# Attention products of two heads in the two halves of the TensorE array, with a transposed output that is turned back

## Chip, cores, metric

One core of one Trainium2 chip. The metric is the device time of one execution in microseconds, the median of several; every run named below was fast, and each kernel was compared with runs of the kernel before on the same chip.

## The reference

Decaying linear attention over 4 batches, 8 heads, 768 tokens and a head width of 64, in float32; then a Fourier mix over tokens and width, a layer norm and an MLP of 512 - 2048 - 512, whose weights come as float64.

```python
# attention, block by block (the kernel takes blocks of 128, which is the same sum)
intra = (qb @ kb.T * Dmask) @ vb                # Dmask[i, j] = lam ** (i - j), i >= j
inter = (qb * lam ** (pos + 1)) @ kv_state
out   = intra + inter
kv_state = lam ** block * kv_state + (kb * lam ** (block - 1 - pos)).T @ vb
# then, with x = out as (batch, seq, heads * 64)
u  = x + real(fft(fft(x, axis=1), axis=2))
ch = relu(layer_norm(u) @ w_ch1) @ w_ch2
return u + ch
```

## The kernel before

A head is 64 wide and the array is 128 by 128, so the kernel puts two heads (a "pair") into each operand. For the scores the keys stand in a matrix that is half zeros (`kbd`), so that one head's keys meet only that head's queries; the state is block diagonal for the same reason. All products use the whole array.

```python
kb = kbd[(b * NC + c) % 2]                      # zeros outside the two diagonal blocks
for hi in range(2):
    nc.scalar.copy(kb[HD[hi], :, hi, :], ptk[HD[hi]])
...                                             # ptq: queries transposed; qT: VectorE's copy of them
for g in range(2):                              # scores: 128 rows, half of them zeros
    ps = psum_a([C, 4, C])
    for j in range(4):
        hp, hi = divmod(4 * g + j, 2)
        nc.tensor.matmul(ps[:, j, :], lhsT=kb[:, hp, hi, :], rhs=qT[:, hp, :], ...)
    nc.vector.tensor_tensor(t, ps, decay[:, 4 * g:4 * g + 4, :], op=ALU.mult)
...                                             # state update, 128x128 of which two 64x64 are used
po = psum_a([C, DM])                            # output: tokens on the partitions
for hp in range(HP):
    if c > 0:
        nc.tensor.matmul(po[:, 128 * hp:128 * hp + 128], lhsT=qs[:, hp, :], rhs=s_old[:, hp, :], ...)
    for hi in range(2):
        h = 2 * hp + hi
        nc.tensor.matmul(po[:, D * h:D * h + D], lhsT=sc[h // 4][:, h % 4, :], rhs=vt[:, h, :], ...)
x = xs[b, c] = new(xp, [C, DM], "x")
nc.scalar.copy(x, po)
...                                             # "folds" of x on VectorE and GpSimd, input of the mix
```

The weights are converted from float64 words block by block, five VectorE operations each, during the attention of the first two batches. And a scheduler fixes the order of instructions on every engine at build time, and in the traces VectorE and ScalarE work through their lists in that order.

Of the kernel before, what the change touches and what calls it, by code (L numbers as in the profile page):

```python
# [10 lines left out]
F32 = mybir.dt.float32  # L11
U32 = mybir.dt.uint32
AF = mybir.ActivationFunctionType
ALU = mybir.AluOpType

EPS = 1e-6
# upper words of 2 ** -127 and 2 ** 128 as float64, read as float32
F64_UNDER, F64_OVER = (float(x) for x in np.array([896 << 20, 1151 << 20], np.uint32).view(np.float32))


def _consts(S, DM):
    """DFT tables; they depend on the sequence length and the model width alone."""
    half, nk = S // 2, S // 4 + 1
    s = np.arange(half)
    k1 = np.stack([2 * np.arange(nk), 2 * np.arange(nk) + 1])
    ang = 2.0 * np.pi * ((s[:, None, None] * k1[None]) % S) / S
    # [s in chunk, cos | sin, chunk of s, parity of k1, k1 // 2]
    cs = np.stack([np.cos(ang), np.sin(ang)]).reshape(2, half // 128, 128, 2, nk)
    cs = cs.transpose(2, 0, 1, 3, 4)

    h = DM // 2
    d = np.arange(h)
    k2 = np.arange(DM)
    ang = 2.0 * np.pi * ((d[:, None] * k2[None]) % DM) / DM
    # rows 0..h-1: cos; row h: cos of d = DM/2; rows h+1..: -sin
    dt = np.concatenate([np.cos(ang), -np.sin(ang)])
    dt[h] = np.where(k2 % 2 == 0, 1.0, -1.0)
    dt = dt.reshape(DM // 128, 128, DM).transpose(1, 0, 2)

    # sign of a row under k1 -> S - k1, in the chunk that starts with d = DM/2  # L40
    sgn = -np.ones((128, 1))
    sgn[0] = 1.0

    def c(m):
        return np.ascontiguousarray(m).astype(np.float32)

    return dict(cs=c(cs), dt=c(dt), sgn=c(sgn))
# [3 lines left out]
def kernel(  # L51
# [10 lines left out]
    nc = tc.nc  # L62
    B, H, S, D = q.shape
    DM = H * D
    DFF = moe_w_ch1.shape[1]
    C = 128                 # tokens per attention chunk
    NC = S // C
    HC = NC // 2
    HP = H // 2
# [3 lines left out]
    HM = DM // 2  # L73
    G = 2                   # token tiles per MLP group
    NG = NC // G
    HD = [slice(0, 64), slice(64, 128)]
# [3 lines left out]
    const = ctx.enter_context(tc.tile_pool(name="const", bufs=1))  # L80
# [13 lines left out]
    def new(pool, shape, tag, **kw):  # L94
        cnt[0] += 1
        return pool.tile(shape, F32, tag=tag, name=f"{tag}{cnt[0]}", **kw)

    def psum_a(shape):
        return new(pa, shape, "pa")
# [3 lines left out]

# [1 line left out]
    z = const.tile([H, 2 * C], F32, name="z")  # L105
# [4 lines left out]
    n, b2 = 1, 0  # L110
    while n < C:
# [3 lines left out]
        n, b2 = 2 * n, b2 + 1  # L115
# [3 lines left out]
    z0 = zd[0:1, 0:1]  # L119
    # qpow[(h % 2, d), h // 2, i] = lam_h ** (i + 1)  # L120
    qpow = const.tile([128, HP, C], F32, name="qpow")
# [7 lines left out]
    make_identity(nc, ident)  # L129
    # decay[j, h, i] = lam_h ** (i - j) for i >= j, else 0: rows of z shifted by one each,  # L130
    # read with the partitions reversed and turned round on the tensor engine
    flip = fp.tile([128, 128], F32, tag="fb", name="flip")
# [11 lines left out]

    kbd = [const.tile([128, HP, 2, C], F32, name=f"kbd{i}") for i in range(2)]
    st = [const.tile([128, HP, 128], F32, name=f"st{i}") for i in range(2)]
    for t in kbd + st:
        nc.gpsimd.memset(t, 0.0)

# [1 line left out]
    cs = const.tile([128, 2, HC, 2, NK], F32, name="cs")  # L151
# [15 lines left out]
    def load_weights(dst, src):  # L167
        """float64 words -> the nearest float32; below float32's range -> 0."""
        if src.dtype == F32:
            nc.sync.dma_start(dst, src)  # L170
            return
        raw = hp_.tile([128, 2 * WP], U32, tag="hr", name=f"raw{cnt[0]}")
        pe = hp_.tile([128, WP], U32, tag="hr", name=f"pe{cnt[0]}")
        cnt[0] += 1
        nc.sync.dma_start(raw, src.bitcast(U32))
        lo, hi = raw[:, 0:2 * WP:2], raw[:, 1:2 * WP:2]
        lof, hif = lo.bitcast(F32), hi.bitcast(F32)
        d = dst.bitcast(U32)
        # the upper word's magnitude, held between the words of 2 ** -127 and 2 ** 128
        nc.scalar.activation(dst, hif, AF.Abs)  # L180
        nc.vector.tensor_scalar(dst, dst, F64_OVER, F64_UNDER, op0=ALU.min, op1=ALU.max)  # L181
        # sign, exponent and the mantissa's upper 20 bits
        nc.vector.tensor_scalar(pe, d, 0x07FFFFFF, 3, op0=ALU.bitwise_and, op1=ALU.logical_shift_left)  # L183
        nc.vector.scalar_tensor_tensor(d, d, 0x40000000, pe, op0=ALU.bitwise_and, op1=ALU.bitwise_or)  # L184
        nc.vector.scalar_tensor_tensor(d, hi, 0x80000000, d, op0=ALU.bitwise_and, op1=ALU.bitwise_or)  # L185
        # the lower 32 bits, times the power of two
        nc.vector.tensor_scalar(pe, d, 0xFF800000, None, op0=ALU.bitwise_and)
        nc.scalar.activation(lof, lo, AF.Copy, scale=2.0 ** -52)
        nc.gpsimd.tensor_tensor(lof, lof, pe.bitcast(F32), op=ALU.mult)  # L189
        nc.gpsimd.tensor_tensor(dst, dst, lof, op=ALU.add)  # L190
# [9 lines left out]

# [1 line left out]
    xs, folds = {}, {}  # L202

    def pair(t, hp):
        return t[:, 2 * hp:2 * hp + 2, :].rearrange("p a d -> p (a d)")

    def attn_chunk(b, c):
# [13 lines left out]
        for hp in range(HP):  # L221
            nc.tensor.transpose(ptk[:, hp, :], pair(kt, hp), ident)  # L222
        kb = kbd[(b * NC + c) % 2]
        for hi in range(2):
            nc.scalar.copy(kb[HD[hi], :, hi, :], ptk[HD[hi]])  # L225
        ptq = psum_a([128, HP, C])
# [7 lines left out]
        yield 1.2  # L234

        sc = []
        for g in range(2):
            ps = psum_a([C, 4, C])
            for j in range(4):
                hp, hi = divmod(4 * g + j, 2)  # L240
                nc.tensor.matmul(ps[:, j, :], lhsT=kb[:, hp, hi, :], rhs=qT[:, hp, :],  # L241
                                 start=True, stop=True)
            t = new(at, [C, 4, C], "sc", bufs=3)
            nc.vector.tensor_tensor(t, ps, decay[:, 4 * g:4 * g + 4, :], op=ALU.mult)  # L244
            sc.append(t)
            yield 0.9

        s_old, s_new = st[(c + 1) % 2], st[c % 2]
        if not last:
            pu = psum_a([128, HP, 128])  # L250
            for hp in range(HP):
                nc.tensor.matmul(pu[:, hp, :], lhsT=pair(kd, hp), rhs=pair(vt, hp), start=True, stop=True)  # L252
            for hi in range(2):
                o, u = s_new[HD[hi], :, HD[hi]], pu[HD[hi], :, HD[hi]]
                if c == 0:
                    nc.vector.tensor_copy(o, u)
                else:
                    nc.gpsimd.tensor_tensor(o, s_old[HD[hi], :, HD[hi]],
                                            spow[HD[hi]].broadcast_to([D, HP, D]), op=ALU.mult)
                    nc.vector.tensor_tensor(o, o, u, op=ALU.add)  # L260
            yield 0.9

        po = psum_a([C, DM])
        for hp in range(HP):
            if c > 0:
                nc.tensor.matmul(po[:, 128 * hp:128 * hp + 128], lhsT=qs[:, hp, :], rhs=s_old[:, hp, :],  # L266
                                 start=True, stop=False)
            for hi in range(2):
                h = 2 * hp + hi
                nc.tensor.matmul(po[:, D * h:D * h + D], lhsT=sc[h // 4][:, h % 4, :], rhs=vt[:, h, :],  # L270
                                 start=(c == 0), stop=(c == 0 or hi == 1))
        x = xs[b, c] = new(xp, [C, DM], "x")
        nc.scalar.copy(x, po)  # L273

        # fold of the width (d with DM - d), then of the sequence (s with s + S/2)
        if c == 0:
# [11 lines left out]

# [1 line left out]
    uts = {}  # L290
# [56 lines left out]

# [1 line left out]
    def mlp(b):  # L349
# [28 lines left out]

# [1 line left out]
    def front(b):  # L380
# [7 lines left out]
    def weave(lead, other, ratio):  # L388
        """All of lead, and of other what takes ratio times its time."""
        t_lead = t_other = 0.0  # L390
        for d in lead:
            t_lead += d
            while t_other < t_lead * ratio:
                d = next(other, None)
                if d is None:
                    return t_lead + run(lead)
                t_other += d
        return t_lead
# [40 lines left out]
```

## Time and profile before

| | kernel before |
|---|---|
| median of 4 runs | 1050.11 us (1048.64 to 1053.53) |
| span of the profiled run | 1049.2 us |
| TensorE busy / idle in that span | 975.4 / 73.8 us |
| dense period (mix of batch 2 to mix of batch 3) | 522.86 to 757.35 = 234.5 us |
| span less two dense periods ("remainder") | 580.2 us |
| first long MLP block | 229.54 us |

The lines are in the prediction, which tells two regimes apart: the start, up to about 230 us, and the stretch after it, in which TensorE is never idle. The dense period measures the second regime: it holds one MLP and one batch's attention and mix. The remainder measures the start, together with the MLP that has no attention beside it.

### The profile page before, as it was taken

How to read it: one execution, taken by the hardware profiler on the slowest of the kernel's cores; microseconds unless marked ns; L12 is line 12 of the kernel's file. 1: busy time of each engine (PE TensorE's matmuls, PEld its weight loads, DVE VectorE, ACT ScalarE, POOL GpSimd, SP SyncE). 2: the span in 40 equal slices, each digit the busy share in tenths (PEclk: the TensorE clock that was granted, in tenths of full speed). 3: DMA queues.
4: the chain of work that ended last, by engine and by line, in shares of the span. 5: the costliest groups of instructions: out<-in, count | busy, mean ns of one | idle time of the engine just before them, and what ended most of it. 6: DMA issues, size and time to landing. Idle time of an engine off the chain costs nothing.

```text
span 1049.2 us, 10095 instructions
## 1 busy us (share of the span) xinstructions
PE 975.4 (93%) x4116; PEld 686.0 (65%) x4116; DVE 343.7 (33%) x590; ACT 141.3 (13%) x279; POOL 187.4 (18%) x199
## 2 busy tenths in 40 slices
PE   5667667699999999999999999999999999999998
PEld 4666346677574756967965756967865756757573
DVE  5888889970001221223202221322202211000010
ACT  2313222321000100110110100110100100100000
POOL 4557556850000000112200000101200000000000
PEclk8779888899999999999999999999999999999999
DMA  9554324610000001112100001121000000000000
GB/s 235 151 131 121 100 93 129 171 51 1 21 0 11 11 0 41 31 41 71 41 0 21 1 1 40 40 48 34 1 1 20 1 1 20 1 21 1 20 1 20
DMA packets 85037, 45.61 MB, mean 43 GB/s; under 512 B 76024, under 2 KB 77568, under 8 KB 84736
## 3 DMA queue, kind: packets, MB, share of 16 engines
q1 hardware_dynamic: 84992, 44.98, 15.8%
q8 instruction: 32, 0.52, 0.2%
q14 instruction: 13, 0.11, 0.0%
HBM read 38.67 MB, written 6.30 MB: 43 GB/s over the span
## 4 chain that ended last, share of the span: by engine, by line
PE 81%; DVE 4%; issue 1%; POOL 0%; ACT 0%; DVEq 0%; POOLq 0%
PE pm L370 31%; PE pm L356 31%; PE pa L325 6%; PE pa L241 3%; PE pa L298 3%; PE pa L270 2%; PE pa L266 1%; PE pa L252 1%; PE pa L344 1%; PE pa L228 1%; PE pa L222 1%; DVE pe L183 1%; DVE w L184 1%; DVE w L181 0%; DVE w L185 0%
## 5 line engine op out<-in xcount | busy, mean ns | idle before, releaser
L356 PE MATMUL pm<-ut,w 128*128 128x256 f32 x1536 | 343.9, 380 | 0.0
L370 PE MATMUL pm<-w,hr 128*128 128x512 f32 x768 | 337.8, 592 | 0.0
L356 PEld LDWEIGHTS pm<-ut,w 128*128 128x128 f32 x1536 | 288.7, 190 | 46.1 <-issue 9.5
L370 PEld LDWEIGHTS pm<-w,hr 128*128 128x128 f32 x768 | 144.1, 190 | 165.2 <-issue 164.5
L362 DVE TENSOR_SCALAR hr<-pm 128x256 f32<-128x256 f32 x96 | 40.8, 425 | 214.7 <-PE pm L356 214.0
L364 ACT ACTIVATE hr<-pm 128x256 f32<-128x256 f32 x96 | 36.7, 383 | 486.8 <-PE pm L356 422.0
L241 PE MATMUL pa<-qT,kbd 128*128 128x128 f32 x384 | 62.5, 325 | 39.0 <-DVE qT L230 35.0
L241 PEld LDWEIGHTS pa<-qT,kbd 128*128 128x128 f32 x384 | 59.5, 236 | 47.2 <-issue 32.0
L375 DVE TENSOR_TENSOR x<-pm,x 128x512 f32<-128x512 f32 x24 | 16.6, 692 | 188.2 <-PE pm L370 187.9
L335 POOL TENSOR_SCALAR ve<-mv 128x2 f32<-128x2 f32 x12 | 3.6, 297 | 348.1 <-DVE mv L331 348.1
L270 PE MATMUL pa<-v,sc 128*128 128x64 f32 x384 | 54.6, 272 | 0.0
L218 POOL TENSOR_TENSOR kd<-k,decay 128x512 f32<-128x512 f32 x20 | 23.6, 1178 | 166.8 <-PE pa L252 163.0
L270 PEld LDWEIGHTS pa<-v,sc 128*128 128x128 f32 x384 | 52.4, 201 | 0.1
L189 POOL TENSOR_TENSOR raw<-raw,pe 128x512 f32<-128x512 f32 x32 | 42.7, 1334 | 53.0 <-issue 18.4
L328 DVE TENSOR_TENSOR x<-pa,x 128x512 f32<-128x512 f32 x24 | 16.6, 690 | 101.3 <-PE pa L325 101.3
L244 DVE TENSOR_TENSOR sc<-pa,decay 128x512 f32<-128x512 f32 x48 | 32.9, 688 | 43.8 <-PE pa L241 39.8
L325 PE MATMUL pa<-dt,y 128*128 128x512 f32 x96 | 44.4, 606 | 0.0
L190 POOL TENSOR_TENSOR w<-w,raw 128x512 f32<-128x512 f32 x32 | 43.9, 1373 | 2.1
L325 PE MATMUL pa<-dt,yr 128*128 128x512 f32 x96 | 43.3, 595 | 0.0
L225 ACT COPY kbd<-pa 64x512 f32<-64x512 f32 x48 | 27.8, 579 | 93.1 <-PE pa L222 92.2
L266 PE MATMUL pa<-st,qs 128*128 128x128 f32 x160 | 35.1, 302 | 0.0
L273 ACT COPY x<-pa 128x512 f32<-128x512 f32 x24 | 14.1, 586 | 152.8 <-PE pa L270 152.8
(63 smaller groups left out, 686.1 us busy)
## 6 DMA issues: line engine op xcount, KB each, us to landing
raw<-in_moe_w_ch_dram SPq DMA_DIRECT2D x32, 512.0 KB, 3.8
k<-in_k_dram SPq DMA_DIRECT2D x24, 256.0 KB, 3.2
q<-in_q_dram SPq DMA_DIRECT2D x24, 256.0 KB, 4.8
v<-in_v_dram SPq DMA_DIRECT2D x24, 256.0 KB, 3.1
out_dram<-x SPq DMA_DIRECT2D x24, 256.0 KB, 2.0
cs<-k_cs SPq DMA_DIRECT2D x1, 1158.0 KB, 6.5
dt<-k_dt SPq DMA_DIRECT2D x1, 1024.0 KB, 7.8
shifted<-zd SPq DMA_DIRECT2D x1, 512.0 KB, 5.6
```

Of the source, the lines that this page charges most:

```text
L189: nc.gpsimd.tensor_tensor(lof, lof, pe.bitcast(F32), op=ALU.mult)
L190: nc.gpsimd.tensor_tensor(dst, dst, lof, op=ALU.add)
L241: nc.tensor.matmul(ps[:, j, :], lhsT=kb[:, hp, hi, :], rhs=qT[:, hp, :], start=True, stop=True)
L244: nc.vector.tensor_tensor(t, ps, decay[:, 4 * g:4 * g + 4, :], op=ALU.mult)
L266: nc.tensor.matmul(po[:, 128 * hp:128 * hp + 128], lhsT=qs[:, hp, :], rhs=s_old[:, hp, :], start=True, stop=False)
L270: nc.tensor.matmul(po[:, D * h:D * h + D], lhsT=sc[h // 4][:, h % 4, :], rhs=vt[:, h, :], start=(c == 0), stop=(c == 0 or hi == 1))
L298: nc.tensor.matmul(ps[:, n, :], lhsT=f[:, t, cols], rhs=cs[:, trig, t, n, :], start=(t == 0), stop=(t == HC - 1))
L325: nc.tensor.matmul(ps, lhsT=ys[c][rev][:, 128 * tt:128 * tt + 128], rhs=dt[:, c, :], start=(c == 0), stop=(c == KO - 1))
L356: nc.tensor.matmul(ps, lhsT=w1[:, c, 128 * fc:128 * fc + 128], rhs=ut[:, c, :], start=(c == 0), stop=(c == KO - 1))
L362: nc.vector.tensor_scalar(t, ps, 0.0, None, op0=ALU.max)
L364: nc.scalar.activation(t, ps, AF.Relu)
L370: nc.tensor.matmul(ps, lhsT=hr[fc // 4][:, fc % 4, 128 * i:128 * i + 128], rhs=w2[:, fc, :], start=(fc == 0), stop=(fc == FO - 1))
```

## The change

The intent is to give each half of the array its own head: no zeros multiplied, two products side by side. The scores use two tiles of 64 rows, the update two of 64 columns, the state product two of 64 by 64. The output of sc times V has to be transposed for that (the two heads' widths on the partitions), so it is copied and turned back by four transposes per chunk.

```diff
-        kb = kbd[(b * NC + c) % 2]
-        for hi in range(2):
-            nc.scalar.copy(kb[HD[hi], :, hi, :], ptk[HD[hi]])
+        kT = new(at, [128, HP, C], "kT", bufs=2)
+        nc.scalar.copy(kT, ptk)
...
+        pss = [psum_a([C, HP, C]) for _ in range(2)]
+        for hp in range(HP):
+            for hi in range(2):
+                mm(pss[hi][:, hp, :], lhsT=kT[HD[hi], hp, :], rhs=qT[HD[hi], hp, :], start=True, stop=True)
... (decay products for each half; state update, same pattern, into pu[HD[hi], hp, :])
+        po = psum_a([128, HP, C])
+        if c > 0:
+            for hp in range(HP):
+                for hi in range(2):
+                    mm(po[HD[hi], hp, :], lhsT=s_old[HD[hi], hp, :], rhs=qs[HD[hi], hp, :], ...)
+        for hp in range(HP):
+            for hi in range(2):
+                mm(po[HD[hi], hp, :], lhsT=vt[:, 2 * hp + hi, :], rhs=sc[hi][:, hp, :], ...)
+        oT = new(at, [128, HP, C], "oT")
+        nc.scalar.copy(oT, po)
+        px = psum_a([C, HP, 128])
+        for hp in range(HP):
+            nc.tensor.transpose(px[:, hp, :], oT[:, hp, :], ident)
         x = xs[b, c] = new(xp, [C, DM], "x")
-        nc.scalar.copy(x, po)
+        nc.scalar.copy(x, px.rearrange("p h e -> p (h e)"))
```

More of the change, by code (lines that the diff above doesn't have):

```diff
@@ L143 @@
     nc.gpsimd.memset(mhalf, -0.5)
-    kbd = [const.tile([128, HP, 2, C], F32, name=f"kbd{i}") for i in range(2)]
-    st = [const.tile([128, HP, 128], F32, name=f"st{i}") for i in range(2)]
-    for t in kbd + st:
-        nc.gpsimd.memset(t, 0.0)
+    st = [const.tile([128, HP, D], F32, name=f"st{i}") for i in range(2)]
     cs = const.tile([128, 2, HC, 2, NK], F32, name="cs")
@@ L234, in attn_chunk @@
         yield 1.2
-        sc = []
-        for g in range(2):
-            ps = psum_a([C, 4, C])
-            for j in range(4):
-                hp, hi = divmod(4 * g + j, 2)
-                nc.tensor.matmul(ps[:, j, :], lhsT=kb[:, hp, hi, :], rhs=qT[:, hp, :],
-                                 start=True, stop=True)
-            t = new(at, [C, 4, C], "sc", bufs=3)
-            nc.vector.tensor_tensor(t, ps, decay[:, 4 * g:4 * g + 4, :], op=ALU.mult)
+        mm = nc.tensor.matmul
+        pss = [psum_a([C, HP, C]) for _ in range(2)]
@@ L245, in attn_chunk @@
+        for hp in range(HP):
+            for hi in range(2):
+                mm(pss[hi][:, hp, :], lhsT=kT[HD[hi], hp, :], rhs=qT[HD[hi], hp, :], start=True, stop=True)
+        sc = []
+        for hi in range(2):
+            t = new(at, [C, HP, C], "sc", bufs=3)
+            nc.vector.tensor_tensor(t, pss[hi], decay[:, hi::2, :], op=ALU.mult)
             sc.append(t)
-            yield 0.9
+        yield 1.5
         s_old, s_new = st[(c + 1) % 2], st[c % 2]
         if not last:
-            pu = psum_a([128, HP, 128])
+            pu = psum_a([128, HP, D])
@@ L251, in attn_chunk @@
             for hp in range(HP):
-                nc.tensor.matmul(pu[:, hp, :], lhsT=pair(kd, hp), rhs=pair(vt, hp), start=True, stop=True)
-            for hi in range(2):
-                o, u = s_new[HD[hi], :, HD[hi]], pu[HD[hi], :, HD[hi]]
-                if c == 0:
-                    nc.vector.tensor_copy(o, u)
-                else:
-                    nc.gpsimd.tensor_tensor(o, s_old[HD[hi], :, HD[hi]],
-                                            spow[HD[hi]].broadcast_to([D, HP, D]), op=ALU.mult)
-                    nc.vector.tensor_tensor(o, o, u, op=ALU.add)
@@ L261, in attn_chunk @@
-            yield 0.9
-        po = psum_a([C, DM])
-        for hp in range(HP):
-            if c > 0:
-                nc.tensor.matmul(po[:, 128 * hp:128 * hp + 128], lhsT=qs[:, hp, :], rhs=s_old[:, hp, :],
-                                 start=True, stop=False)
-            for hi in range(2):
-                h = 2 * hp + hi
-                nc.tensor.matmul(po[:, D * h:D * h + D], lhsT=sc[h // 4][:, h % 4, :], rhs=vt[:, h, :],
-                                 start=(c == 0), stop=(c == 0 or hi == 1))
+                for hi in range(2):
+                    h = 2 * hp + hi
+                    mm(pu[HD[hi], hp, :], lhsT=kd[:, h, :], rhs=vt[:, h, :], start=True, stop=True)
@@ new lines, in attn_chunk @@
+            if c == 0:
+                nc.vector.tensor_copy(s_new, pu)
+            else:
+                nc.gpsimd.tensor_tensor(s_new, s_old, spow.broadcast_to([128, HP, D]), op=ALU.mult)
+                nc.vector.tensor_tensor(s_new, s_new, pu, op=ALU.add)
+            yield 0.9
+        po = psum_a([128, HP, C])
+        if c > 0:
+            for hp in range(HP):
+                for hi in range(2):
+                    mm(po[HD[hi], hp, :], lhsT=s_old[HD[hi], hp, :], rhs=qs[HD[hi], hp, :],
+                       start=(hp == 0), stop=False, skip_group_check=True)
@@ L272, in attn_chunk @@
+        for hp in range(HP):
+            for hi in range(2):
+                mm(po[HD[hi], hp, :], lhsT=vt[:, 2 * hp + hi, :], rhs=sc[hi][:, hp, :],
+                   start=(c == 0 and hp == 0), stop=(hp == HP - 1), skip_group_check=True)
+        oT = new(at, [128, HP, C], "oT")
+        nc.scalar.copy(oT, po)
+        yield 2.0
+        px = psum_a([C, HP, 128])
+        for hp in range(HP):
+            nc.tensor.transpose(px[:, hp, :], oT[:, hp, :], ident)
         x = xs[b, c] = new(xp, [C, DM], "x")
-        nc.scalar.copy(x, po)
+        nc.scalar.copy(x, px.rearrange("p h e -> p (h e)"))
```

## The prediction

> **What bounds the kernel now.** I read the page first: busy shares, the 40 slices, then the costliest groups.
>
> ```profile
> PE 975.4 (93%) x4116; PEld 686.0 (65%) x4116; DVE 343.7 (33%) x590; ACT 141.3 (13%) x279; POOL 187.4 (18%) x199
> PE   5667667699999999999999999999999999999998
> DVE  5888889970001221223202221322202211000010
> PEclk8779888899999999999999999999999999999999
> ```
>
> There are two regimes. In the first eight or nine slices (26 us each, so about 225 us) VectorE is eight or nine tenths busy and TensorE only six or seven, on a granted clock of 0.7 to 0.8. After that TensorE is never idle and everything else is. The table of windows puts figures on it:
>
> ```profile
> 15.00:95.00 80.00, 53.03 (x325) 48.05 (x324) 67.43 (x94) 22.50 (x39) 49.98 (x46) 0.77 0.62 165
> 152.00:218.00 66.00, 47.48 (x332) 44.41 (x330) 61.60 (x91) 21.09 (x36) 45.67 (x43) 0.86 0.55 145
> 640.00:700.00 60.00, 60.00 (x315) 47.62 (x313) 15.75 (x30) 8.78 (x18) 6.24 (x9) 1.00 0.17 40
> ```
>
> (Columns: window, length, then busy PE, PE load, DVE, ACT, POOL, then clock, DMA share, GB/s.) The order of instructions on TensorE explains it. The scheduler runs the attention of batches 0 and 1 at the start, beside the conversion of the weights; those 12 chunks of 128 tokens are the "front". The attention of batches 2 and 3, 12 more chunks, is sprinkled between MLP products from 411 us on; those are the "dense" chunks, where every nanosecond of TensorE counts. From 880 us on only MLP is left and nothing can change.
>
> In the timeline of a dense chunk, the pitch of the products is the distance from a block's start to the next block's start, over its count (an fp32 product is recorded as two passes, each with its weight load; a transpose as one):
>
> ```profile
> 424.86 1.97 PEld L270 LDWEIGHTS pa<-v,sc 128*128 128x128 f32 x16
> 425.07 1.89 PE L270 MATMUL pa<-v,sc 128*128 128x64 f32 x16
> 426.81 3.67 PE L356 MATMUL pm<-ut,w 128*128 128x256 f32 x16
> 434.64 1.05 PE L241 MATMUL pa<-qT,kbd 128*128 128x128 f32 x8
> 435.54 1.89 PE L356 MATMUL pm<-ut,w 128*128 128x256 f32 x8
> ```
>
> L270 takes (426.81 - 425.07)/16 = 109 ns a pass although only 64 columns stream; L241 takes 0.90/8 = 112 ns with 128 columns. So 128 columns of weights or 128 streamed columns both cost about 110 ns, whichever is larger. (L356, 256 columns, takes 7.01/32 = 219 ns.)
>
> In the front, the timeline's waits show who holds TensorE:
>
> ```profile
> 56.14 3.75 PE L241 MATMUL pa<-qT,kbd 128*128 128x128 f32 x16 [7.13 <-DVE qT L230]
> 70.70 3.75 PE L241 MATMUL pa<-qT,kbd 128*128 128x128 f32 x16 [5.67 <-DVE qT L230]
> 185.66 2.02 PE L241 MATMUL pa<-qT,kbd 128*128 128x128 f32 x16 [2.06 <-DVE qT L230]
> ```
>
> Each chunk's scores wait 2 to 7 us for one VectorE copy, which is queued behind weight conversion. That is slack which a longer TensorE chain may eat.
>
> **What the Trainium skill says.** (1) "TensorEngine Tiling (Array Packing)", Key Properties: tiles run loads and products independently, but changing the tiling mode drains the engine. The trace shows what that may cost. Before has a one-column product among full ones:
>
> ```profile
> 523.84 1.14 PE L298 MATMUL pa<-cs,fo 128*128 128x193 f32 x6
> 524.91 1.14 PE L298 MATMUL pa<-cs,fe 128*1 128x193 f32 x6
> 524.91 0.74 PEld L298 LDWEIGHTS pa<-cs,fe 128*1 128x1 f32 x6 [0.23 <-PE pa L298]
> 525.89 1.14 PE L298 MATMUL pa<-cs,fo 128*1 128x193 f32 x6
> 526.96 7.17 PE L356 MATMUL pm<-ut,w 128*128 128x256 f32 x32
> ```
>
> Six equal passes take 525.89 - 524.91 = 0.98 us inside a form, 1.07 us up to a change of form: 0.09 us for the drain. The new form's first weight load is not pulled ahead either (0.23 us of idle loader), so it is exposed. (2) "TensorE: Matmul & The Clock Gate", LDWEIGHTS: time goes with the columns, columns/1.2 ns, so 107 for 128 and 53 for 64; the 109 ns of L270 agrees. (3) Same page, Part 3, Measured speedup vs the span model: 3.07 times for four row tiles, 2.38 for three column tiles, at 512 streamed columns. No run yet shows it for two-pass fp32 products of 64 or 128 columns. (4) Same page, Part 1: an idle TensorE drops to half clock for some 3.4 us. It agrees: 16 L241 passes take 3.75 us in the front where 8 take 0.90 when dense.
>
> **The change part by part, dense chunks.** Per batch, before: 48 transposes, 96 passes of scores, 40 of the state update, 40 of the state product, 96 of sc times V: 320 x 0.11 = 35.2 us. After: 72 transposes (24 more, turning back), 96 score passes (64 rows, 128 weight columns), 80 update passes (64 weight columns, 64 streamed), 80 state passes and 96 sc-V passes (64 weight columns, 128 streamed): 424. The halves of the array now hold different heads.
>
> - *Nothing overlaps:* 72, 96, 80 and 96 at 0.11 and 80 at 0.055 = 42.2 us, +7 per batch, +14 for two.
> - *Streams overlap, but a load waits for the pass before it in program order:* two passes of one head, then two of the other; over four passes 0.107 + 0.055 + 0.107 + 0.055, so 0.081 each for state and sc-V, scores bound by loads at 0.11: 37.2 us, +4 for two.
> - *Streams overlap, loads go one at a time:* state and sc-V at 0.055: 32.6 us, -5 for two.
> - *Loads overlap too:* scores 0.055, update 0.028: 25.1 us, -20 for two.
>
> On top come changes of mode, which before has none of in its attention. From the order of the changed kernel I count 37 per batch: 15 back to the full array, 6 into scores, 5 into the update, 5 into the state product, 6 into sc-V. 37 x 0.09 = 3.3; exposed loads 21 x 0.107 + 16 x 0.053 = 3.1; together 6.4 us per batch, 13 for two. So dense: +27, +17, +8 or -7 us.
>
> **Front.** VectorE loses one of two state operations per chunk (0.42 us each, ten chunks: -4 us) and GpSimd one of two decay multiplications (0.68 us, eight chunks: -5 us), which also slows VectorE less where both run. ScalarE has three copies of 0.59 us as before, but one of them (transposed output) now sits in TensorE's chain: products, copy, back-transposes, and only then the next chunk's transposes, because TensorE keeps program order. Per chunk: copy and its two handovers 0.9, transposes 0.44 to 0.9, mode changes about 1.2, passes -1.7 to +1.2: about +2 us, against the 2 to 7 us of slack. VectorE has filler (one or two weight blocks of about 4 us per chunk), so I let a third through: 12 x 0.7 = +8. The mix of batch 1 (L298, 60 passes of 0.163 = 9.8 us) moves behind the first MLP block, onto the full clock: before it held TensorE from about 212 to 228 us, with stalls, so some -4. Front sum: -4 + 8 - 4 = 0, from -12 (full overlap) to +12 (none).
>
> **The rivals.** (a) Full concurrency: 1051 - 7 - 12 = about 1032. For it: the skill's figures; against it: the passes are short, and the loads (110 ns for 128 columns) are as long as the streams. (b) Loads bind, streams overlap: 1051 + 8 to 17 + 0 = 1059 to 1068. For it: before is already load-bound at L270. (c) No concurrency for fp32: 1051 + 27 + 12 = 1090. For it: nothing in the trace, only that before never runs two products at once. (d) The front is bound by its chain instead of VectorE, as ScalarE's copy waits behind a weight activation which waits for its load (that wait totals 38 us): +10 to +20 on any of these. For it: ScalarE is strictly in order in the listing; against: the scheduler kept filler beside most of these waits.
>
> **Range and chances.** Weights 0.33 for (a), 0.25 and 0.3 for the two forms of (b) (1059, 1068), 0.12 for (c): 341 + 265 + 320 + 131 = 1057; I round to 1056. The 2% lines are 1030 and 1072. Only the good end of (a), helped by the front, passes the first: 0.13. (c), and (b) with some of (d), pass the second: 0.25. Within: 0.62. Range 1030 to 1082.
>
> **What would show it.** In a dense chunk: 16 score passes in 0.9 us (a) or 1.8 us (b, c); 16 sc-V passes in 0.9, 1.3 or 1.8 us; about 0.1 to 0.2 us at every change of form; no TensorE idle outside the front. In the front: TensorE waiting for ScalarE's copy before L276; the end of the front (first long MLP block) still between 218 and 240 us, VectorE still above 85%. I am wrong if mode changes turn out free, if the back-transposes stall dense chunks, or if the front moves by more than 12 us.

## More of the kernel before

Runs of one kernel still differ: in the first call of the experiments the kernel before took 1048.64 to 1053.4 us, the shortest at a granted TensorE clock of 0.967 of the full one and the longest at 0.962. Differences of 2 or 3 us between single profiled runs are to be read with this in mind.

## The result, and the profile after

The changed kernel takes 1045.9 us (median of 4 runs, 1045.06 to 1048.09), against 1050.11. The ratio is the mean time of one kernel's fast runs over that of the other's of the same rounds, so not quite the ratio of these medians: 0.9956, 95% interval 0.9936 to 0.9976. It is 0.44% faster. The prediction said 1056, 0.5% slower: the measured time is inside its range, but the sign is wrong.

From the page of the changed kernel (busy totals, then the 40 slices):

```profile
PE 961.4 (92%) x4532; PEld 644.9 (62%) x4532; DVE 321.1 (31%) x570; ACT 140.6 (13%) x279; POOL 174.3 (17%) x179
PE   4568667579999999999999999999999999999998
DVE  5888777960011221212301221222212221000010
```

TensorE is busy for 961.4 us, 14.0 less than before, although it runs 416 more instructions. The span fell only from 1049.2 to 1046.3, so its idle time rose from 73.8 to 84.9 us. The slices say where: from the tenth on TensorE is full in both kernels.

The table of windows of the changed kernel (window, length, busy PE, PE load, DVE, ACT, POOL, then clock, DMA share, GB/s):

```profile
152.00:218.00 66.00, 43.68 (x410) 37.06 (x410) 58.86 (x87) 20.87 (x36) 44.50 (x38) 0.71 0.55 148
640.00:700.00 60.00, 60.00 (x377) 43.22 (x375) 13.92 (x27) 8.25 (x17) 5.88 (x8) 1.00 0.18 40
```

In the dense window TensorE is busy throughout, as before. In the window of the start VectorE is busy for 58.86 us (before 61.60), TensorE for 3.80 us less, and its granted clock fell from 0.86 to 0.71. The two kernels are not at the same work in this window, so the difference in VectorE's time is no measure of what was saved; that can be read from its state operations, 20 of 0.42 us before and 10 of 0.41 after in the start, 8.3 and 4.1 us.

**Dense part: gained.** The dense period runs from 534.47 to 764.81 us: 230.3, that is 4.15 less, or -8.3 for two batches. The timeline of TensorE in dense chunks of the changed kernel:

```profile
651.35 1.16 PE L237 MATMUL pa<-qT,kT 64*128 64x128 f32 x16
652.44 3.72 PE L361 MATMUL pm<-ut,w 128*128 128x256 f32 x16
656.09 0.69 PE L252 MATMUL pa<-v,kd 128*64 128x64 f32 x16
656.71 1.99 PE L361 MATMUL pm<-ut,w 128*128 128x256 f32 x8
...
658.63 1.09 PE L269 MATMUL pa<-sc,v 128*64 128x128 f32 x16
659.66 3.72 PE L361 MATMUL pm<-ut,w 128*128 128x256 f32 x16
...
663.65 3.62 PE L361 MATMUL pm<-ut,w 128*128 128x256 f32 x16
667.11 0.60 PE L219 MATMUL pa<-ident,k 128*128 128x128 f32 x4
...
677.08 1.09 PE L265 MATMUL pa<-qs,st 64*64 64x128 f32 x16
678.11 1.09 PE L269 MATMUL pa<-sc,v 128*64 128x128 f32 x16
```

Take the distance from one block's start to the next, not the recorded lengths, which overlap. The record of a form's first product starts together with its weight load (both at 651.35 us for the scores), so this load counts in its own block. The 16 score passes cost 652.44 - 651.35 = 1.09 us. With everything overlapped they would take 16 x 0.055 = 0.88, plus the exposed first load 0.107, plus the drain 0.09: 1.08. The state product takes 1.03 and sc times V 1.03 (0.88 + 0.053 + 0.09 = 1.02), the update 0.62 (16 x 0.028 + 0.053 + 0.09 = 0.59). A block of 16 MLP passes between full-array work takes 667.11 - 663.65 = 3.46 us, one between two tiled families 656.09 - 652.44 = 3.65: 0.19 more, again 0.107 + 0.09. So the prediction's rival (a), full concurrency with paid changes of mode, describes every family here within 0.03 us.

**Start: lost.** The remainder went from 580.2 to 585.6 us: +5.4. (The profiled run of the changed kernel was the longest of its four, 1048.09 us against a median of 1045.9. By the ratio of the times, -4.6 us in all, the start lost about 3.7.) The ends of the start on TensorE, first in the kernel before:

```profile
213.31 0.56 PE L270 MATMUL pa<-v,sc 128*128 128x64 f32 x4
...
227.82 1.88 PE L325 MATMUL pa<-dt,y 128*128 128x512 f32 x4
229.54 6.64 PE L356 MATMUL pm<-ut,w 128*128 128x256 f32 x30
```

and in the changed kernel:

```profile
207.49 0.60 PE L224 MATMUL pa<-ident,q 128*128 128x128 f32 x4
213.17 2.08 PE L237 MATMUL pa<-qT,kT 64*128 64x128 f32 x16 [5.08 <-ACT raw L185]
...
221.24 0.90 PE L276 MATMUL pa<-ident,oT 128*128 128x128 f32 x3 [0.73 <-ACT oT L272]
221.93 14.23 PE L361 MATMUL pm<-ut,w 128*128 128x256 f32 x60
```

The MLP starts 7.6 us earlier, which looks like a gain. But before, the mix of batch 1 was by then done up to its first D products: 9.8 us in L298 (60 passes of 0.163) and 229.54 - 227.82 = 1.7 in L325. In the changed kernel this lies behind the first MLP block (304 to 331 us), where TensorE has no idle time to hide it in. 11.5 - 7.6 = 3.9 us of the 5.4 are accounted for so; I did not place the other 1.5, which lie within the scatter of single runs. The attention of batch 1 ends at 221.9 instead of 213.7 us, and with it the mix moved.

These 8.2 us did not arise in one place. The mix of batch 0 begins at 82.18 us, 2.9 earlier than before (85.12). From there to the first transposes of batch 1 it takes 70.65 us instead of 66.28, +4.4, and the six chunks of batch 1 take 69.10 instead of 62.31, +6.8. So the chunks of batch 0 gained, and part of the loss arose in a mix, where no scores wait for a query copy. Only the last chunk of batch 1 is looked at closely here.

Before the scores of the last chunk TensorE waits 5.08 us. (The releaser printed there, ScalarE, is the wait's last semaphore event; the query copy L226 below ended at 213.02, just ahead of the start at 213.17.) Summed over the six chunks of batch 1 these waits were 13.8 us before and 17.3 after. In batch 0 they went the other way, from 25.2 to 17.7, so over the whole start they fell from 39.0 to 35.0. VectorE's timeline in the same chunk:

```profile
207.12 1.56 DVE L178 TENSOR_SCALAR w<-w 128x512 f32<-128x512 f32 x1 [0.16 <-ACT w L177]
208.78 1.31 DVE L180 TENSOR_SCALAR pe<-w 128x512 uint32<-128x512 uint32 x1
...
210.74 0.42 DVE L286 TENSOR_TENSOR fb<-x 128x255 f32<-128x255 f32 x1
...
211.67 0.42 DVE L287 TENSOR_TENSOR fb<-x 128x255 f32<-128x255 f32 x1
212.01 0.42 DVE L184 TENSOR_SCALAR pe<-w 128x512 uint32<-128x512 uint32 x1
212.34 0.68 DVE L226 COPY qT<-pa 128x512 f32<-128x512 f32 x1
```

The transposed queries were ready at about 208.1 us. VectorE is not idle, but in its fixed order a whole conversion block (L178 to L184) and the folds of the previous chunk (L286, L287) stand before the query copy (L226). Those folds now need x, which is there only after the products, a copy, the turning back and a second copy. The kernel before in the same chunk, where the queries were ready at 202.8 us:

```profile
203.14 1.43 DVE L185 SCALAR_TENSOR_TENSOR w<-raw,w 128x512 uint32<-128x512 uint32 x1
204.50 0.41 DVE L281 TENSOR_TENSOR fb<-x 128x255 f32<-128x255 f32 x1
204.83 0.41 DVE L187 TENSOR_SCALAR pe<-w 128x512 uint32<-128x512 uint32 x1
205.17 0.41 DVE L282 TENSOR_TENSOR fb<-x 128x255 f32<-128x255 f32 x1
205.61 0.69 DVE L230 COPY qT<-pa 128x512 f32<-128x512 f32 x1
```

There, too, the folds and part of a conversion block stand before the query copy (L230). What the changed kernel adds in this chunk is two more conversion operations in front of it. That the change first brought the folds ahead of the copy is therefore not so.

This gave two theories. A: ScalarE's copy between products and turning back, for which TensorE waits 0.73 us in each of 12 chunks of the start (8.7 us in all), sits in its in-order chain. B: the folds, available later, hold back the next query copy together with a conversion block.

### The profile page after: what moved, and what is told of

It reads as the page before. It is cut to its first block, busy times and chain, and to the rows that moved or that the text cites. A ratio compares the mean times of both kernels' runs of the same rounds, so it can differ in the third digit from the quotient of the medians.

```text
span 1046.3 us, 10861 instructions
## 1 busy us (share of the span) xinstructions
PE 961.4 (92%) x4532; PEld 644.9 (62%) x4532; DVE 321.1 (31%) x570; ACT 140.6 (13%) x279; POOL 174.3 (17%) x179
## 3 DMA queue, kind: packets, MB, share of 16 engines
q1 hardware_dynamic: 84992, 44.98, 15.8%
## 4 chain that ended last, share of the span: by engine, by line
PE 81%; DVE 4%; issue 1%; ACT 0%; POOL 0%; DVEq 0%; ACTq 0%
PE pm L361 32%; PE pm L375 32%; PE pa L330 6%; PE pa L303 3%; PE pa L237 2%; PE pa L269 2%; PE pa L265 1%; PE pa L252 1%; PE pa L276 1%; PE pa L349 1%; DVE pe L180 1%; DVE w L178 1%; PE pa L219 1%; PE pa L224 1%; DVE w L182 0%
## 5 line engine op out<-in xcount | busy, mean ns | idle before, releaser
L237 PE MATMUL pa<-qT,kT 64*128 64x128 f32 x384 | 36.7, 345 | 35.0 <-DVE qT L226 29.9
L237 PEld LDWEIGHTS pa<-qT,kT 64*128 64x128 f32 x384 | 31.4, 242 | 43.7 <-issue 24.8
L330 PE MATMUL pa<-dt,yr 128*128 128x512 f32 x96 | 45.5, 621 | 0.0
L269 PE MATMUL pa<-sc,v 128*64 128x128 f32 x384 | 31.8, 299 | 3.1 <-DVE sc L241 3.1
L349 PE MATMUL pa<-ident,un 128*128 128x128 f32 x96 | 17.0, 306 | 17.9 <-DVE un L345 17.9
L330 PEld LDWEIGHTS pa<-dt,yr 128*128 128x128 f32 x96 | 18.9, 201 | 21.4 <-issue 21.2
L272 ACT COPY oT<-pa 128x512 f32<-128x512 f32 x24 | 14.1, 586 | 131.8 <-PE pa L269 131.8
L330 PEld LDWEIGHTS pa<-dt,y 128*128 128x128 f32 x96 | 18.8, 201 | 21.0 <-issue 20.3
```

Source lines behind the costliest of these rows:

```text
L237: mm(pss[hi][:, hp, :], lhsT=kT[HD[hi], hp, :], rhs=qT[HD[hi], hp, :], start=True, stop=True)
L269: mm(po[HD[hi], hp, :], lhsT=vt[:, 2 * hp + hi, :], rhs=sc[hi][:, hp, :], start=(c == 0 and hp == 0), stop=(hp == HP - 1), skip_group_chec ...
L330: nc.tensor.matmul(ps, lhsT=ys[c][rev][:, 128 * tt:128 * tt + 128], rhs=dt[:, c, :], start=(c == 0), stop=(c == KO - 1))
L349: nc.tensor.transpose(pt[:, c, :], un[:, 128 * c:128 * c + 128], ident)
```

## The experiments

Of each kernel I quote the median, the ratio to the kernel before (95% interval), the dense period and the remainder of its profiled run. The kernel before ran with medians of 1049.59 to 1051.22.

### a_scores: the scores part alone on the kernel before

```diff
-        for hi in range(2):
-            nc.scalar.copy(kb[HD[hi], :, hi, :], ptk[HD[hi]])
+        nc.scalar.copy(kT, ptk)
 ... scores as in the change; state and output as before
```

> The kernel before with the scores alone in the two halves of the array (one key tile of both heads in place of the padded one; state and output as before). Theory (the scores carry the gain of the part where TensorE is always busy, and the transposed output costs the start): one batch in that part falls from 234.5 us to about 231.6 (96 passes at 0.055 saved, 12 changes of form at 0.2 us paid), the start does not get longer, the whole is 1038 to 1043 us. Rival (the gain needs the output part as well): the period stays above 233 us and the whole is 1046 us or more.

Measured: 1054.78 us, ratio 1.0031 [1.0015, 1.0047]. The dense period fell to 231.25 (-3.2), as expected; the remainder rose to 590.8. So the total missed: a shorter dense part and a longer start, as in the whole change. Here nothing is turned back, so the turning back cannot be the only reason of the longer start.

### b_output: the rest of the change, with the old scores

```diff
-                mm(pss[hi][:, hp, :], lhsT=kT[HD[hi], hp, :], rhs=qT[HD[hi], hp, :], start=True, stop=True)
+                nc.tensor.matmul(ps[:, j, :], lhsT=kb[:, hp, hi, :], rhs=qT[:, hp, :], start=True, stop=True)
```

> The changed kernel with the old padded scores: only state update, state product, output and the turning back are changed. Theory: one batch in the busy part gains about 1.2 us over before (233.3), because the 24 transposes and the changes of form take back what the halves save, the start loses 2 to 6 us, the whole is 1047 to 1053 us, level with before. Rival (this part carries the gain): period under 232 us, whole under 1046.

Measured: 1053.34 us, ratio 1.0022 [1.0005, 1.0039], just past the upper edge of the range expected; dense period 233.31 (-1.2), remainder 584.5. The dense parts add up (-3.2 - 1.2 = -4.4 against -4.15), the starts do not (+10.6 and +4.3 against +5.4).

### d_one_half_at_a_time: same products, one half after the other

```diff
-        for hp in range(HP):
-            for hi in range(2):
+        for hi in range(2):
+            for hp in range(HP):
                 mm(pss[hi][:, hp, :], lhsT=kT[HD[hi], hp, :], rhs=qT[HD[hi], hp, :], start=True, stop=True)
 ... and so in the other three families
```

> The changed kernel with the loops over heads and halves turned round: all four products of one half, then all four of the other, in each of the four families. Same products, same forms, same changes of form. Theory (two products overlap only where neighbours in program order lie in different halves): 16 score passes take about 1.9 us in place of 1.09, state product and output likewise; a batch in the busy part goes from 230.3 to 244 to 248 us and the whole to 1080 to 1095 us. Rival (TensorE looks far enough ahead to overlap any of them): 1046 us as the changed kernel.

Measured: 1073.23 us, ratio 1.0227 [1.0199, 1.0255]; dense period 240.38. From its dense timeline:

```profile
665.50 1.71 PE L237 MATMUL pa<-qT,kT 64*128 64x128 f32 x16
667.14 3.72 PE L361 MATMUL pm<-ut,w 128*128 128x256 f32 x16
```

1.64 us for 16 score passes instead of 1.09, so the overlap is real and needs neighbours in different halves. I had expected 1.9, a period of 244 to 248 and a whole of 1080 to 1095, which was too much. The trace shows the reason: where the passes of one half end and those of the other begin, at 666.05, 666.27 and 666.38 us, two passes start within 6 ns of each other; elsewhere one starts every 0.11 us. So some passes at the border still overlap.

### e_no_turning_back (wrong result)

```diff
-        oT = new(at, [128, HP, C], "oT")
-        nc.scalar.copy(oT, po)
 ...
-            nc.tensor.transpose(px[:, hp, :], oT[:, hp, :], ident)
-        nc.scalar.copy(x, px.rearrange("p h e -> p (h e)"))
+        nc.scalar.copy(x, po.rearrange("p h e -> p (h e)"))
```

> The changed kernel without the transposes back (the transposed output is copied straight to x, so the result is WRONG on purpose): one ScalarE copy and four transposes per chunk less. In the busy part 24 x 0.11 = 2.6 us a batch must go (227.7 us), so 5.3 in two batches. Theory (the copy and the transposes lengthen the chain of each chunk at the start and so the start): the first long MLP block begins 6 to 12 us earlier, the whole is 1029 to 1035 us. Rival (the start is held by the conversion of the weights, not by the chain): the start moves by less than 3 us and the whole is 1038 to 1042 us.

Measured: 1037.38 us, ratio 0.9872 [0.9853, 0.989]; dense period 227.70 (-2.6 against the changed kernel: 24 transposes at 0.11), remainder 580.1 (-5.5). The total lies between the two ranges. Turning back costs the start something, but without it the start is no shorter than before the change.

### n_plain_weights_before and n_plain_weights_after: no conversion (wrong result)

The conversion is replaced by one plain copy of the upper words, in both kernels:

```diff
-        nc.scalar.activation(dst, hif, AF.Abs)
-        nc.vector.tensor_scalar(dst, dst, F64_OVER, F64_UNDER, op0=ALU.min, op1=ALU.max)
 ...
+        nc.scalar.copy(dst, hif)
```

> The kernel before with the conversion of the weights cut to one ScalarE copy of the upper words (result WRONG on purpose): VectorE and GpSimd are free for attention at the start, so the chunks at the start run at the length of their own chain. The scheduler then puts only batch 0 at the start and three batches in the busy part. Baseline for the next run; I expect chunks every 8 to 10 us at the start.

> The changed kernel with the same cut (WRONG on purpose). Theory (the changed chunk's own chain is longer, as the copy, the turning back and the changes of form outweigh the shorter products): chunks at the start come 0.5 to 2 us further apart than in the run before, although the three batches in the busy part gain 4.15 us each; the whole is 3 to 10 us shorter than its baseline. Rival (the chain is not longer; the start lost its time only through the interleaving with the conversion): the same or a shorter distance between chunks, the whole 12 us or more shorter than its baseline.

Measured: 985.76 us (ratio 0.938) for the kernel before and 969.59 us (0.9237) for the changed one. The difference is 16.2 us by the medians and 14.1 by the spans of the profiled runs. Three times the 4.15 of a dense batch is 12.5 of it. The rest is not the chunks at the start: from the second chunk's scores to the sixth's it takes 36.2 us before (26.8 to 63.0) and 36.0 after (26.0 to 62.0), and the first MLP block begins at 100.3 and 99.7. So the chunk's own chain is neither longer, as the theory had it, nor measurably shorter where no conversion stands beside it. The prediction had counted on about 2 us more per chunk. This points to the meeting with the conversion rather than to TensorE's chain as such, but does not prove it: the scheduler puts only batch 0 at the start of this pair, and in batch 0 the changed kernel lost nothing with the conversion either.

### f_late_turning_back: turning back, copy and folds after the next chunk's scores

```diff
+        def turn_back():
             px = psum_a([C, HP, 128])
             ... (transposes, copy to x, folds: unchanged, indented)
+        late.append(turn_back())
+        if last:
+            yield from late.pop()
 # and in the next chunk, behind the decay products of its scores:
+        if late:
+            yield from late.pop()
```

> The changed kernel with the turning back of a chunk (transposes, copy to x, folds) issued after the next chunk's scores, so that TensorE does not wait for the ScalarE copy between chunks. Theory (the wait and the transposes in TensorE's order lengthen the start): the attention of batch 1 ends 5 to 10 us earlier and the whole is 1036 to 1042 us, nearly what leaving the turning back out gave less the 5.3 us of its transposes in the busy part. Rival (the conversion of the weights holds the start): within 3 us of the changed kernel, 1043 to 1049 us.

Measured: 1037.06 us (1036.09 to 1038.76), ratio 0.9877 [0.9858, 0.9895], correct. The dense period is unchanged (230.5), the remainder 575.3. The waits before the scores of batch 1 fell to 12.0 us, the mix of batch 1 is back ahead of the first MLP block, which starts at 224.40. Against the changed kernel that is 2.5 us later with 11.5 less left to do: -9.0, and the ratios say -8.3 (0.9877 - 0.9956, of 1050). This is the best version, better than both kernels.

### h_one_more_buffer: a rival, the conversion's buffers

```diff
-    hp_ = ctx.enter_context(tc.tile_pool(name="hp", bufs=FO // 4 + 1))
+    hp_ = ctx.enter_context(tc.tile_pool(name="hp", bufs=FO // 4 + 2))
```

> The changed kernel with six in place of five buffers in the pool through which the weights are converted (each block takes two), same order of products on TensorE. Theory (the chain of the chunks holds the start): same time within 2 us. Rival (the conversion loop, load to ScalarE to VectorE to GpSimd to the next load, holds the start by its few buffers): the long waits of ScalarE for the weights' loads (31 us in all) fall by half and the whole is 4 to 10 us shorter, 1036 to 1042 us.

Measured: 1047.41 us, ratio 0.9975 [0.9958, 0.9993]: no gain over the changed kernel. But ScalarE's wait for the weights' loads fell only from 31.2 to 26.3 us in the first 240 us, not by half as the rival had it, so the run shows that a sixth buffer does not help, and not that a shorter wait would not. It shows something else: the waits before the scores of batch 1 fell to 13.5 us here, as low as before the change (13.8), and the time did not follow. These waits alone do not measure the loss.

### v_less_weights_first: is it scatter of the schedule?

The share of the conversion that is issued beside batch 0 becomes smaller:

```diff
-    t_front = weave(front(0), w, 0.4)
+    t_front = weave(front(0), w, 0.3)
```

> The changed kernel with the share of weight conversion woven into the first attention lowered from 0.4 to 0.3: the same instructions, nearly the same order on TensorE, one or two conversion blocks moved on VectorE. It shows how far the start moves by order alone. If the scatter of the start is an accident of order, the time moves by 3 us or more either way; if the start is held by sums of work, it stays within 2 us of 1046.

Measured: 1045.84 us, ratio 0.9958 [0.9941, 0.9974], as the changed kernel. This change of the order, at least, moves nothing. It does not clear the rival of scatter: over the correct kernels tried here, d aside, the remainder lies between 575.3 and 590.8 us, and the scores of batch 1 begin anywhere from 148.9 (g_after_late_folds) to 160.5 us (a_scores). How much of that is the edits' own and how much accident of the order stays open.

### g_after_late_folds and i_folds_alone_late: theory A or theory B

In the first the transposes stay in place and the copy to x and the folds go late; in the second only the folds do. Both leave TensorE's wait for the transposed output's copy where it was.

```diff
         nc.scalar.copy(x, px.rearrange("p h e -> p (h e)"))
+        def rest():
             ... (folds, unchanged, indented)
+        late.append(rest())
```

> The changed kernel with only the copy to x and the folds issued after the next chunk's scores; the transposes back stay where they were in TensorE's order, right behind the output products. It separates two readings of the gain of the late turning back (9 us). Theory A (TensorE waits for the ScalarE copy between chunks): no gain, 1043 to 1049 us. Theory B (on VectorE the folds, which wait for x, stand with two conversion blocks ahead of the next chunk's query copy, and hold it back): most of the gain is there, 1036 to 1041 us.

> The changed kernel with the folds alone issued after the next chunk's scores; the copy to x stays in its place on ScalarE, right behind the transposes back. The late-folds run moved both. Theory B (the folds' place on VectorE costs the start): same as that run, 1038 to 1043 us. Rival (the second copy's place in ScalarE's queue, ahead of the conversion's first step, costs it): back to 1044 to 1048 us.

Measured: 1040.88 us, ratio 0.9914 [0.9898, 0.993], and 1040.85 us, ratio 0.9914 [0.9898, 0.9931]. Both recover 0.42%, 4.4 us, of the 8.3 of the late turning back; by their profiled runs' remainders (577.0 for the first, against 585.6 and 575.3) it is 8.6 of 10.3. The copy to x makes no difference. VectorE and TensorE of the second, in the chunk shown above:

```profile
200.14 0.43 DVE L180 TENSOR_SCALAR pe<-w 128x512 uint32<-128x512 uint32 x1
200.60 0.69 DVE L181 SCALAR_TENSOR_TENSOR w<-w,pe 128x512 uint32<-128x512 uint32 x1
201.21 0.68 DVE L226 COPY qT<-pa 128x512 f32<-128x512 f32 x1
```

```profile
199.98 0.60 PE L224 MATMUL pa<-ident,q 128*128 128x128 f32 x4
202.04 1.16 PE L237 MATMUL pa<-qT,kT 64*128 64x128 f32 x16 [1.46 <-DVE qT L226]
```

The query copy now interrupts the block instead of following it. TensorE waits 1.46 us instead of 5.08, and the scores run in 1.16 us instead of 2.08, so on the full clock. The attention of batch 1 ends at 208 us. So moving the folds alone gives at least half of what the late turning back recovers; theory A, or whatever else comes with late transposes, keeps at most 4 us by the times and 1.7 by the profiles. Theory B's mechanism is seen in this chunk and in the waits before the scores of batch 1, which fell from 17.3 to 9.5 us. It does not cover the whole gain: the attention of batch 1 ends 13.8 us earlier (208.2 for 221.9), of which 6.0 arose in the mix of batch 0 (64.65 us for 70.65), where no query copy is held back. The edit changes VectorE's whole order, and why the mix gets shorter with it is not shown.

### g_before_late and g_scores_late: the same cure on the other two

The edit is that of g_after_late_folds, on the kernel before and on a_scores:

```diff
+        def rest():
             x = xs[b, c] = new(xp, [C, DM], "x")
             nc.scalar.copy(x, po)
             ... (folds, unchanged, indented)
+        late.append(rest())
```

> The kernel before with the copy to x and the folds issued after the next chunk's scores. In its order on VectorE the folds mostly come behind the next query copy already. Theory B: little to gain, 1046 to 1052 us, so that the late turning back is worth more in the changed kernel than in the one before. Rival (late folds are simply a better order for any version): 1039 to 1044 us.

> The scores-alone kernel (1054.8 us, its busy part 3.2 us a batch faster than before but its start 10 us longer) with the copy to x and the folds issued after the next chunk's scores. Theory B (its long start comes of the order on VectorE, not of the halves): the start falls back to that of before or lower, the whole is 1037 to 1045 us. Rival (something in the scores' products themselves lengthens the start): over 1050 us.

Measured: 1056.83 us, ratio 1.0048 [1.0025, 1.0071], a loss where I expected 1046 to 1052 (four of its six runs took 1056.7 to 1057.4, two, at a higher granted clock, 1051.3 and 1051.8, inside the range; the profiled run is one of the long ones); and 1048.52 us, ratio 0.998 [0.9962, 0.9999], 0.5% better than a_scores but short of the 1037 to 1045 expected. In both the attention of batch 1 ends at 213 to 214 us (in a_scores it was 225) but the conversion only at 243 to 245, and the first MLP blocks, from 237 us on, wait for VectorE. So late folds are no cure by themselves: the start ends with the later of attention and conversion, and the folds' place trades one against the other. Why the conversion comes so late there I did not settle. The expectation for g_before_late also misread the kernel before: in seven of the ten chunks that follow another one in the start's two batches, folds run between the moment at which the queries are ready and their copy.

### l_late_and_buffer: late turning back and the sixth buffer

The two edits of f and h together.

> The late turning back with the sixth conversion buffer: the candidate for the best version. The buffer alone gave nothing to the changed kernel (-0.2% against +-0.2%). If the start is now held by the conversion, it gives 2 to 5 us (1032 to 1035 us); if VectorE's own work holds it, it stays at 1036 to 1039 us.

Measured: 1039.03 us, ratio 0.9889 [0.9871, 0.9908]. No gain over f_late_turning_back.

## Why the prediction was right or wrong

- **The dense model was right, its weights were not.** Rival (a) said -7 for two batches; -8.3 was measured, and every family and every change of mode came out as worked. The failed step is "Weights 0.33 for (a), 0.25 and 0.3 for the two forms of (b) (1059, 1068), 0.12 for (c)": two thirds of the weight were on no or partial concurrency, so that the dense part came to +8 us in the weighted mean (0.33 x -7 + 0.25 x 8 + 0.3 x 17 + 0.12 x 27) where -8.3 was measured. The sceptical rivals fall together: loads of 128 columns overlap too, or 16 score passes could not take 1.09 us. d_one_half_at_a_time reproduces what the sceptical rivals feared, by undoing the order.
- **The start was wrong by sign.** Rival (a) had -12 there. +5.4 was measured. Of the -12, -4 was for the postponed mix, and that was right: before, 11.5 us of work took 213.7 to 229.5, 15.8 us, so moving it saves 4.3. The other -8 was to come from an earlier end of attention, as I read it; the prediction does not split it. The attention of batch 0 did end 2.9 us earlier, but that of batch 1 ended 8.2 us later (213.7 to 221.9), and 8.2 - 4.3 gives the 3.9 us found above.
- **The term that failed in it** is "about +2 us, against the 2 to 7 us of slack", of which a third was let through: a longer chain per chunk, with VectorE's other work as filler that gives way. Without the conversion the chain is not longer at all (36.0 us for 36.2 over four chunks). The slack was misread as well: "Each chunk's scores wait 2 to 7 us" holds for eight of the twelve chunks, the other four wait 0.9 to 1.8. In its place the runs show that the order of VectorE's work beside the conversion matters: moving only the folds, with the turning back and TensorE's wait for ScalarE left as they were (8.7 us), gives back 4.4 us or more. How the change itself made that order worse is only in part shown: the waits before the scores rose in batch 1 (17.3 for 13.8 us) and fell in batch 0 (17.7 for 25.2), 4.4 us were lost in the mix of batch 0, and h_one_more_buffer has short waits and no gain.
- **VectorE's saved 4 us** were there (state operations 4.1 us for 8.3 in the start), but the start as a whole got longer.
- **Rival (d)**, ScalarE's copy in TensorE's chain, was there as seen (0.73 us in each of 12 chunks) but is worth at most 4 us of 8.3. Its longer form, the copy queued behind a weight activation, did not show, though the run with a sixth buffer shortened that wait too little to test it.
- **The central number** (1056) came from averaging rivals that could not all be true; with (a) alone it read 1032. Two misses partly cancelled, -8.3 us in the dense part and +5.4 in the start, so that the measured time lies near the number is luck.
- **Open:** the 1.5 us of the start not placed; how much of the loss is due to the lower granted clock there (0.71 against 0.86), which late folds undo in the chunk shown but which no run isolates; why the mix of batch 0 got 4.4 us longer and, with the folds moved, 6.0 shorter; and why the conversion ends so late in the two kernels with late folds and the old output.

## What to carry to other kernels

Two heads in two halves of the array do run side by side, if neighbours in program order lie in different halves; count about 0.2 us for every change of tiling (0.09 + 0.107, or 0.14 where the new form loads 64 columns), so 0.3 to 0.4 us for an excursion and back, to find out whether it pays. When a change lengthens the path to some secondary work (here the folds), look at the order of the engine that runs it: on an engine that works in order, secondary work can stand before an urgent copy. Issuing it later helped two kernels here (-0.4% and -0.5%) and hurt a third (+0.5%), so it has to be tried each time, and the kernel before looked at in the same place. A phase that ends earlier is not a gain before one has checked what moved out of it.

## What the Trainium skill lacked or had wrong

- "TensorEngine Tiling (Array Packing)", Key Properties, says that changing the mode drains the array, without a size. Here: 0.09 us of drain, and the first load of the new mode exposed (0.107 us for 128 columns); a block of 16 MLP passes between two tiled families takes 3.65 us instead of 3.46.
- "TensorEngine Tiling (Array Packing)", Gotcha 1, says that different row tiles cannot access the same PSUM bank simultaneously. The 64 by 64 tiles of the state product write the two partition halves of one bank, 16 passes in 1.03 us, overlapped, with a correct result. For disjoint partitions the sentence is too strict.
- No page has figures for the concurrency of fp32 products in two passes with 64 or 128 columns. Here both halves overlap fully, loads included: 16 score passes take 1.09 us, against 1.64 with one half after the other.
